# A fused attention and gated-MLP kernel: the first chunk's second half turned by TensorE, and the last chunk's logits in one burst

## The chip, the cores and the metric

The kernel runs on one core of one Trainium2 chip. The metric is the time of one execution on the device in microseconds (us). Engines: PE is TensorE, DVE is VectorE, ACT is ScalarE, POOL is GpSimd, SP is the engine that issues most DMAs here. A q after an engine's name (PEq, SPq) is its instruction queue, which issues DMAs and waits. "Span" is the time in the trace from the first to the last instruction; it is about 1.8 us shorter than the measured time.

Names in the profile: a timeline line gives the output tile first, then its inputs. `lps` are the logits, `e` the exponentials, `eD` their copy in DRAM, `A` the copy loaded back, `m` the mixes, `o` the attention output; `psf<-o,wo` is the output projection, `psf<-hT,wd` the down-projection of the MLP, `psg` and `psu` its gate and up products. "glu" is the gated MLP.

## The reference, cut to what matters

```
x: 2048 x 640 (bf16)
xn = layernorm(x)
q, k, v = xn @ wqkv                    # 32 heads of 20
logits[s, w] = q[s] . k[s - 2 w] / sqrt(20)   for w = 0..7, masked where s - 2 w < 0
o[s] = sum over w of softmax(logits[s])[w] * v[s - 2 w]
out = x + o @ wo + ((xn @ w_gate) * (xn @ w_up)) @ w_down      # inner width 1536
```

Each token attends to eight earlier ones, two apart. The products q*k and A*v are therefore elementwise and run on DVE; the projections and the MLP run on PE.

## The kernel before

The 2048 tokens are cut into four chunks of 512 (numbered 0 to 3), held transposed (features on partitions). A small list scheduler at build time (`Plan`) gives every task an engine, an estimated duration, needs, and a priority; it decides the order on each engine. The order is then fixed.

Chunk 0 has to start fast, so before the change all of it is loaded already transposed, in two halves of 256 tokens. The layer norm statistics of a half are sums over partitions, done by PE with a matrix of ones: S is the sum of x, V the sum of squares of the centred x. (Only here and in "S and V sums" is V this sum; "V's weights", "V starts" and "V of chunk 0" mean the projection to v.)

```
    def feature_sums(what, h, tiles):          # S (what="xt") and V (what="sq") of half h
        ...
            for i in tiles:
                nc.tensor.matmul(st[0]["sum", what, h][:], lhsT=ones[:], rhs=st[0][what, h][:, i, :], ...)

    def center(h, lo, hi): ...                 # DVE: xd = x - mean
    def squares(h, lo, hi): ...                # ACT: xd * xd
    def first(h, j, hi, i=None): ...           # PE: q, k projections of xd (not yet scaled)
    def first_scaled(h, j): ...                # DVE: PSUM * rstd -> q, k
    def normalized(h): ...                     # DVE: xd * rstd -> xnT, for v and the MLP
```

Attention of a chunk: four products of q and k (DVE), four folds (DVE), logits (PE), exponentials (ACT), `e` stored to DRAM and loaded back broadcast over partitions as `A` (the DMA round trip), four mixes A*v and three sums (DVE), then `o` in two DVE operations, then the output projection `outer` on PE. For the last chunk, the logits were made in two bursts, each followed by its own half of `e` and `A`; for the others in one:

```
        for g in range(2):
            if c == NCH - 1:
                add("pe", ("logits", c, g), logits(c, g), 0.45, [("pw", c, 2 * g + 1), ("pw", c, 2 * g), ("sel",)], prio=-100,
                    ring="lg", until=("exp", c, g), slack=0.8)
            elif g == 1:
                add("pe", ("logits", c, 1), lambda: (logits(c, 0)(), logits(c, 1)()), 0.7,
                    [("pw", c, n) for n in range(W // 2)] + [("sel",)], prio=-100,
                    ring=("lg", "aux"), until={"lg": ("exp", c, 0), "aux": ("exp", c, 1)}, slack=0.8)
            add("act", ("exp", c, g), exps(c, g), 0.6, [("logits", c, g if c == NCH - 1 else 1)], prio=-100)
            ...
            add("sp", ("kept e", c, g), keep_e(c, g), 0.65, [done], prio=-100, kb=128)
            add("sp", ("A", c, g), load_a(c, g), 0.65, [("kept e", c, g)] + ([("A", c, 0)] if g else []), prio=-100, kb=512, ...)
```

The softmax here doesn't subtract the row's maximum and nothing guards it: scores larger than these inputs give would overflow.

## Time and profile before

| | before |
|---|---|
| time, median of 3 runs | 258.36 us (258.36 to 258.64) |
| span in the trace | 256.7 us |
| PE busy | 251.0 us, 98% |
| DVE busy | 228.7 us, 89% |
| what PE waited for, in all | 1.0 us |

The page of the kernel before, its busy times and the chain of work that ended last:

```profile
span 256.7 us, 3323 instructions
...
PE 251.0 (98%) x1274; PEld 119.4 (47%) x1297; DVE 228.7 (89%) x233; ACT 110.2 (43%) x203; POOL 31.0 (12%) x55
...
PE 98%; issue 1%; DVE 0%
```

The list of waits of the kernel before, PE only (engine, line, released by whom: us in total, times, longest):

```profile
PE wps L126 <- PEq L844: 0.8, 1, 0.8
PE psf L734 <- issue: 0.2, 1, 0.2
```

PE waits for nobody after its start. The time is the sum of the PE instructions' slots. DVE, busy 89%, sets nothing here. (A slot is the time from one matmul's start to the next one's; the timeline's second column is the modelled duration, which overlaps with the next.)

The timeline of PE at the start of the kernel before. The columns are start, duration, engine, line, operation, output and input, shape, number of instructions:

```profile
8.26 0.49 PE L261 MATMUL sum_sq<-sq,ones 128*128 128x256 bf16 x3
...
9.13 0.71 PE L261 MATMUL sum_xt<-x_115,ones 128*128 128x256 bf16 x5
9.68 0.71 PE L321 MATMUL ps_143<-x_115,wqkv 128*128 128x256 bf16 x5
...
12.95 0.71 PE L261 MATMUL sum_sq<-sq,ones 128*128 128x256 bf16 x5
...
17.87 5.56 PE L443 MATMUL ps<-xnT,wqkv 128*128 128x512 bf16 x24
23.27 1.24 PE L694 MATMUL psg<-xnT,wgu 128*128 128x512 bf16 x5
```

The two groups of five sums at 9.13 and 12.95 are the second half's S and V. From 8.26 to the first gate matmul of the MLP at 23.27 there is no gap.

The timelines of DVE, then of PE, then of SP's DMA issues, at the end of the kernel before:

```profile
215.50 2.82 DVE L624 TENSOR_TENSOR m<-v,A 128x5120 bf16<-128x5120 bf16 x1
...
228.39 2.83 DVE L624 TENSOR_TENSOR m<-v,A 128x5120 bf16<-128x5120 bf16 x1 [2.67 <-DMA A<-eD]
...
242.59 1.49 DVE L643 TENSOR_TENSOR o<-o,R 128x2560 bf16<-128x2560 bf16 x1
```

```profile
218.40 0.40 PE L535 MATMUL lps<-f,sel 128*32 128x512 bf16 x4
233.54 1.24 PE L739 MATMUL psf<-o,wo 128*128 128x512 bf16 x5
247.60 2.75 PE L739 MATMUL psf<-o,wo 128*128 128x512 bf16 x11
```

```profile
219.48 0.57 SPq L556 DMA_DIRECT2D eD<-e  x1
...
224.05 0.56 SPq L568 DMA_DIRECT2D A<-eD  x1
```

DVE already mixes with the first half of A at 215.50, before the second logits at 218.40. It waits 2.67 us for the second half, and still finishes `o` at 244.1, 3.5 us before PE asks for it at 247.60. The two output projections at 233.54 and 247.60 are 14.06 us apart. The same work lies between them in all kernels, so what this distance has over 14.06 is the time that PE waited for `o`.

### The profile page before, as it was taken

The numbers are of one execution on the slowest core, as the hardware profiler recorded it, in microseconds if no ns is written. First come the engines' busy times: TensorE is split into PE (matmuls) and PEld (weight loads), VectorE is DVE, ScalarE is ACT, GpSimd is POOL, SyncE is SP. The second block draws the span as 40 slices with busy tenths as digits, with TensorE's granted clock in tenths as the row PEclk, the third lists the DMA queues.
The fourth block names the chain that finished last, engine by engine and source line by source line (L and its number), as shares of the span: only waits on it lengthen the run. The fifth ranks groups of instructions, "written<-read, shape, count | busy, mean of one in ns | idle before, by whom it ended". The sixth has DMA issues, their size and how long they took to land.

```text
span 256.7 us, 3323 instructions
## 1 busy us (share of the span) xinstructions
PE 251.0 (98%) x1274; PEld 119.4 (47%) x1297; DVE 228.7 (89%) x233; ACT 110.2 (43%) x203; POOL 31.0 (12%) x55
## 2 busy tenths in 40 slices
PE   8999999999999999999999999999999999999994
PEld 4884444444444444444444444444444444444462
DVE  2599999999989999899898999899999999959913
ACT  3516855588755550184555550105555400550000
POOL 0310040000000141223100301302000014000000
PEclk9999999999999999999999999999999999999999
DMA  6993299004570010246350000146002014230003
GB/s 222 414 435 136 111 235 382 17 0 153 182 204 3 0 41 0 82 125 220 113 102 4 0 0 22 54 152 221 11 3 82 0 41 150 82 102 0 23 0 103
DMA packets 16496, 27.11 MB, mean 106 GB/s; under 512 B 9456, under 2 KB 12160, under 8 KB 16096
## 3 DMA queue, kind: packets, MB, share of 16 engines
q1 hardware_dynamic: 13680, 14.98, 18.6%
q0 software_dynamic: 2368, 11.33, 12.0%
q10 hardware_dynamic: 432, 0.59, 0.6%
q8 instruction: 10, 0.16, 0.3%
q14 instruction: 6, 0.05, 0.1%
HBM read 19.16 MB, written 5.77 MB: 97 GB/s over the span
## 4 chain that ended last, share of the span: by engine, by line
PE 98%; issue 1%; DVE 0%
PE ps L443 21%; PE psf L734 20%; PE psg L694 20%; PE psu L694 20%; PE psf L739 8%; PE wps L126 1%; PE lps L535 1%; PE sum_xt L261 1%; PE ps_141 L321 1%; PE ps_143 L321 0%; PE ps_145 L321 0%; PE ps_147 L321 0%; PE ps_279 L321 0%; PE ps_267 L321 0%; PE ps_230 L321 0%
## 5 line engine op out<-in xcount | busy, mean ns | idle before, releaser
L694 PEld LDWEIGHTS <-wgu 128*128 128x128 bf16 x480 | 46.6, 98 | 56.4 <-issue 0.5
L694 PE MATMUL psu<-xnT,wgu 128*128 128x512 bf16 x232 | 59.2, 379 | 0.4
L694 PE MATMUL psg<-xnT,wgu 128*128 128x512 bf16 x238 | 59.5, 379 | 0.1
L734 PE MATMUL psf<-hT,wd 128*128 128x512 bf16 (+1 forms) x247 | 54.0, 369 | 0.4 <-issue 0.2
L624 DVE TENSOR_TENSOR m<-v,A 128x5120 bf16<-128x5120 bf16 x16 | 45.1, 2818 | 2.7 <-DMA A<-eD 2.7
L508 DVE TENSOR_TENSOR pw<-q,k 128x5120 bf16<-128x5120 bf16 (+1 forms) x20 | 45.5, 2277 | 0.3
L443 PE MATMUL ps<-xnT,wqkv 128*128 128x512 bf16 x170 | 39.5, 379 | 0.3
L700 ACT CAST us<-psu 128x512 bf16<-128x512 f32 x48 | 28.1, 586 | 26.8 <-PE psu L694 26.6
L734 PEld LDWEIGHTS <-wd 128*128 128x128 bf16 x252 | 24.3, 98 | 27.5 <-issue 0.8
L700 ACT CAST gs<-psg 128x512 bf16<-128x512 f32 x48 | 28.1, 585 | 19.2 <-PE psg L694 18.8
L634 DVE TENSOR_TENSOR m<-m 128x5120 bf16<-128x5120 bf16 x12 | 33.8, 2819 | 0.1
L443 PEld LDWEIGHTS <-wqkv 128*128 128x128 bf16 x175 | 17.0, 98 | 20.6 <-issue 0.4
L739 PE MATMUL psf<-o,wo 128*128 128x512 bf16 (+1 forms) x103 | 24.1, 369 | 0.1
L714 DVE TENSOR_TENSOR hT<-gs,us 128x512 bf16<-128x512 bf16 x48 | 19.6, 422 | 4.2 <-ACT us L700 4.1
L761 POOL DMA_DIRECT2D out<-osb x15 | 8.2, 549 | 108.1 <-DVE osb L756 108.0
L544 ACT ACTIVATE e<-lps 128x512 bf16<-128x512 f32 x8 | 4.5, 598 | 35.9 <-PE lps L535 35.9
L519 DVE TENSOR_TENSOR pw<-pw 128x2048 bf16<-128x2048 bf16 x16 | 19.5, 1219 | 0.1
L443 PE MATMUL ps<-xnT,wa 128*128 128x512 bf16 x74 | 17.6, 379 | 0.1
L464 ACT CAST v<-ps 128x512 bf16<-128x512 f32 x20 | 11.7, 585 | 12.5 <-PE ps L443 12.5
L739 PEld LDWEIGHTS <-wo 128*128 128x128 bf16 x105 | 10.3, 98 | 11.3
L453 POOL COPY v<-v 128x70 bf16<-128x70 bf16 x3 | 5.9, 1955 | 54.8 <-DVE m L624 54.8
L464 ACT CAST k<-ps 128x512 bf16<-128x512 f32 x15 | 8.8, 586 | 7.8 <-PE ps L443 7.8
(87 smaller groups left out, 173.9 us busy)
## 6 DMA issues: line engine op xcount, KB each, us to landing
A<-eD SPq DMA_DIRECT2D x8, 512.0 KB, 4.7
x_c<-x SPq DMA_DIRECT2D x3, 640.0 KB
wgu<-wgu POOLq DMA_DIRECT2D x1, 1920.0 KB, 11.3
xnD<-x_c SPq DMA_DIRECT2D x3, 640.0 KB, 3.1
wd<-wd POOLq DMA_DIRECT2D x1, 1920.0 KB, 8.1
xr<-xT POOLq DMA_DIRECT2D x15, 128.0 KB, 2.4
out<-osb POOLq DMA_DIRECT2D x15, 128.0 KB, 2.1
wgu<-wgu POOLq DMA_DIRECT2D x1, 1280.0 KB, 8.7
```

The lines of the kernel that those rows point to most:

```text
L443: nc.tensor.matmul(ps[:, 0 : hi - lo], lhsT=weight(b, i), rhs=s["xnT"][:, i, lo:hi], start=(i == 0), stop=(i == KT - 1),)
L464: nc.scalar.copy(dst[:, t, o + lo : o + hi], s["ps", b, lo][:, 0 : hi - lo])
L508: nc.vector.tensor_tensor(s["pw", n][:, :, :, lo:hi], s["q"][:, None, :, lo:hi].to_broadcast([P, 2, KT, hi - lo]), pairs(s["k"][:, :, off ...
L519: nc.vector.tensor_tensor(t[:, :, 0:2, :], t[:, :, 0:2, :], t[:, :, 2:4, :], ALU.add)
L624: nc.vector.tensor_tensor(s["m", n][:], pairs(s["v"][:, :, off : off + CS], DIL), s["A"][:, 2 * n : 2 * n + 2, None, :].to_broadcast([P, 2 ...
L634: nc.vector.tensor_tensor(b[:], a[:], b[:], ALU.add)
L694: nc.tensor.matmul(ps[:], lhsT=wgu[:, f, r, i, :], rhs=st[c]["xnT"][:, i, :], start=(i == 0), stop=(i == KT - 1))
L700: nc.scalar.copy(t[:], st[c]["gps", f, r][:])
L714: nc.vector.tensor_tensor(h[:], st[c]["gu", f, 0][:], st[c]["gu", f, 1][:], ALU.mult)
L734: nc.tensor.matmul(ps[:], lhsT=wd[:, f, m * P : (m + 1) * P], rhs=st[c]["h", f][:, lo:hi], start=(f == 0), stop=False)
L739: nc.tensor.matmul(st[c]["psf", m, lo][:], lhsT=wo[:, t, m * P : (m + 1) * P], rhs=st[c]["o"][:, t, lo:hi], start=False, stop=(t == KT - 1))
L761: eng.dma_start(out=out[c, m, :, lo:hi], in_=st[c]["osb", m][:, lo:hi])
```

## The change

The intent has two parts. First, the second half of chunk 0 is loaded as rows, with its statistics on DVE (`bn_stats`), normalized in place and then turned by ten PE transposes (128 columns each). That removes ten 256-column sums from PE, and takes the PSUM scaling of that half from DVE; its products can start earlier. Second, the last chunk's logits are made in one burst of eight matmuls, which cost less than two bursts of four.

```diff
-        ("sp", nc.sync, ("x0", 1, 0), None, (1, 0, 5), None, 320),
+        ("sp", nc.sync, ("xc", 0), None, None, None, 320),          # rows of the second half, and the identity
...
+    for j in range(KT):
+        add("pe", ("pe C", j), lambda j=j: [first(1, j, n, i) for n in range(2) for i in range(KT)], 1.09,
+            [("turned", 0), ("wb", 2), ("pe v0", 0, 4)], prio=-895 + 0.1 * j, ring="mm", until=("qk1", j), slack=0.3)
+        add("act", ("qk1", j), first_moved(1, j), 0.57 if j < KT - 1 else 0.72, [("pe C", j)], prio=-800)
+
+    def turn_block(k):
+        def emit():
+            ps = (ps_log if k else ps_aux).tile([P, KT, P], BF, name="turned", tag="lg" if k else "aux")
             for i in range(KT):
+                nc.tensor.transpose(ps[:, i, :], st[0]["x", k][:, tcols(i)], st[0]["eye"])
+            st[0]["t", k] = ps
+        return emit
+
+    def turned_moved(k):
+        return lambda: nc.scalar.copy(st[0]["xnT"][:, :, HF + k * P : HF + (k + 1) * P], st[0]["t", k][:])
...
+    for h in range(2):                                               # V of chunk 0, now in halves
+        for t, n in ((0, 2), (2, 2), (4, 1)):
+            add("pe", ("pe v0", h, t), values0(h, t, n), 0.55 * n, [("wv",), ("turned", 0) if h else ("xn0",), ...
...
         for g in range(2):
-            if c == NCH - 1:
-                add("pe", ("logits", c, g), logits(c, g), 0.45, [("pw", c, 2 * g + 1), ("pw", c, 2 * g), ("sel",)], prio=-100,
-                    ring="lg", until=("exp", c, g), slack=0.8)
-            elif g == 1:
+            if g == 1:
                 add("pe", ("logits", c, 1), lambda: (logits(c, 0)(), logits(c, 1)()), 0.7,
-                    [("pw", c, n) for n in range(W // 2)] + [("sel",)], prio=-100,
+                    folded + [("sel",)], prio=-100,
                     ring=("lg", "aux"), until={"lg": ("exp", c, 0), "aux": ("exp", c, 1)}, slack=0.8)
-            add("act", ("exp", c, g), exps(c, g), 0.6, [("logits", c, g if c == NCH - 1 else 1)], prio=-100)
+            add("act", ("exp", c, g), exps(c, g), 0.6, [("logits", c, 1)], prio=-100)
```

(Cut: the removal of the second half's sums, centring and scaling; products and folds of chunk 0 in halves; renamings.) In the order on PE, V's first half and the transposes now come right after the first half's q and k.

## The prediction

> **What bounds the kernel now.** TensorE. The busy table gives PE 251.0 us of a 256.7 us span at full clock; the timeline shows no PE gap from the first sums (3.57 us) to the end of the last output projection (about 253.1). The list of waits has PE waiting 1.0 us in all. DVE is busy 89%, but nobody on PE waits for it. So only two things change the time: the sum of PE instruction slots, and new PE gaps.
>
> **PE slots (start to start in the timeline).** A 128x512 matmul takes 0.216 us (five in 1.08), a 128x256 one 0.109.
> - Removed: the second half's feature sums and sums of squares, 10 x 0.109 = 1.09 us.
> - Added: ten 128x128 transposes. The Trainium skill, "TensorE: Matmul & The Clock Gate", section "Wait — 56ns, not 53.3ns?", gives 55.6 ns for 128 columns; this trace has no such matmul, but its 0.109 and 0.216 fit the same rule. Estimate 0.6 us.
> - V of chunk 0 in halves: 50 x 0.1091 instead of 25 x 0.2158, +0.06 us.
> - Last chunk's logits: two bursts of four cost 0.43 us each; a burst of eight (chunk 1) costs 0.64. Saves 0.2 us.
> Sum: about -0.65 us.
>
> **New gaps at the start.** The second half's S and V sums, and its projections, kept PE busy while weights landed. Now PE wants the third projection block at 9.68 us, but POOL's copies show its weights landing at about 10.0, and V's weights at 11.95; V now comes at about 11.3 instead of 17.9. The new load is 32 KB larger. Estimate: two gaps, 0.75 us together. The row statistics, the transposes and their evictions should just keep up. The glu starts near 23.4 us (before 23.27). Front: about +0.1 after its slots.
>
> **The other engines.** DVE loses the second half's centring, scaling of PSUM and normalizing (6.5 us), gains statistics and one scaling (2.4 us) and about 2 us from folding chunk 0 in halves. It starts chunk 0's products some 4 us earlier, so the scheduler puts logits and down-projections earlier; the PE order shows this. I expect DVE to keep up with small or no PE gaps.
>
> **The end.** Before, the last chunk's first half of A was loaded at 194.6 us, long before its second logits (218.40). Two mixes and a sum ran while the second half travelled; DVE still waited 2.67 us for it (mix at 228.39, 10.0 us after the logits) and finished o at 244.1, 3.5 us before PE asked for it (247.60). Now all four mixes come after the single burst. By PE order, 33.7 us of PE work lies between that burst and the last output projection. The chain is: logits to first A landing 10.0 to 10.9 us; then DVE in its new order, seven 128x5120 ops, o, five gates, one residual, 24.6 us. That is 35.1 us, so PE should stall about 1.4 us before the last output projection.
>
> **Total.** -0.65 + 0.75 + 1.4 = +1.5 us, about 259.9; I lean down a little since landings and gaps may be kinder: 259.4 us, range 257.5 to 261.2. Faster by over 2%: 0.02; within: 0.94; slower: 0.04.
>
> **What would show it.** Gaps on PE at about 9.7 and 11.5 us released by the weight DMA; transposes near 56 ns apart; DVE waiting for A before the last chunk's first mix, at about 224 us; PE waiting 1 to 2 us for o before the last output projection; nothing else idle on PE.
>
> **What would make it wrong.** A landing faster, or the burst earlier on PE than I counted (no end stall: about 258.4); transposes costing 0.1 us or more; PE waiting for folds at the earlier chunks' logits (DVE slack there shrinks to 1 to 3 us); weights landing earlier than POOL's copies suggest.

## The result and the profile after

| | before | after |
|---|---|---|
| time, median | 258.47 us (258.36 to 258.64, 4 runs) | 258.78 us (258.72 to 258.88, 4 runs) |
| ratio, 95% interval | | 1.0012, 0.9995 to 1.0029 |
| span in the trace | 256.7 us | 256.9 us |
| PE busy | 251.0 us | 250.7 us |
| DVE busy | 228.7 us | 227.6 us |

A ratio is the mean time of one kernel's fast runs over the mean of the other's of the same rounds, so it is not quite the ratio of the medians quoted. The time is the same within 2%, and within 0.3%.

The page of the kernel after, busy times and the chain that ended last:

```profile
span 256.9 us, 3403 instructions
...
PE 250.7 (98%) x1299; PEld 121.2 (47%) x1322; DVE 227.6 (89%) x242; ACT 114.1 (44%) x215; POOL 30.2 (12%) x56
...
PE 82%; DVE 10%; DMA 6%; issue 1%; ACT 0%; DVEq 0%; ACTq 0%
```

The list of waits of the kernel after, PE only:

```profile
PE wps L127 <- PEq L873: 0.8, 1, 0.8
PE sum_xt L278 <- DMA x_115<-x: 0.2, 1, 0.2
PE psf L767 <- DVE o L673: 0.2, 1, 0.2
```

The chain is no longer PE alone: it now runs at the start through the loads (the weights of q, k and v have 3.0% of the span) and at the end through DVE's mixes and the DMA of A, and the list of waits names the spot, the last output projection waiting for `o`. The 10% of DVE does not mean that DVE costs 10%; a chain switches engine as soon as a wait is longer than zero. How much the switch cost is only the length of the wait.

The timeline of PE at the start of the kernel after:

```profile
8.23 0.49 PE L278 MATMUL sum_sq<-sq,ones 128*128 128x256 bf16 x3
8.56 0.71 PE L318 MATMUL ps_142<-x_115,wqkv 128*128 128x256 bf16 x5
9.10 0.71 PE L318 MATMUL ps_144<-x_115,wqkv 128*128 128x256 bf16 x5
9.77 0.72 PE L318 MATMUL ps_146<-x_115,wqkv 128*128 128x256 bf16 x5
...
10.87 0.71 PE L318 MATMUL ps_150<-x_115,wqkv 128*128 128x256 bf16 x5
11.72 1.27 PE L493 MATMUL ps<-xnT,wqkv 128*128 128x256 bf16 x10
12.82 0.44 PE L388 MATMUL turned<-x_c 128*128 128x128 bf16 x5
13.10 0.71 PE L493 MATMUL ps<-xnT,wqkv 128*128 128x256 bf16 x5
...
13.93 1.25 PE L493 MATMUL ps<-xnT,wqkv 128*128 128x256 bf16 x10
15.12 0.71 PE L318 MATMUL ps_293<-xnT,wa 128*128 128x256 bf16 x5
...
23.31 1.24 PE L722 MATMUL psg<-xnT,wgu 128*128 128x512 bf16 x4
```

Read starts, not durations. Five 256-column matmuls take 0.545 us, so the block at 9.10 ends at 9.65 and the next should start there: it starts at 9.77, a gap of 0.13 (the third block of weights had not landed). The block at 10.87 ends at 11.42, V starts at 11.72: 0.30 (V's weights). The ten at 13.93 end at 15.02, the second half's projections start at 15.12: 0.10 (they wait for ACT's copy of the second turned block). The five transposes from 12.82 to 13.10 take 0.28 us, 56 ns each. From the squares at 8.23 to the MLP at 23.31 it is 15.08 us, against 15.01 before: without its three gaps it would be 14.55.

The timelines of DVE, then of PE, then of SP's DMA issues, at the end of the kernel after:

```profile
222.90 2.83 DVE L654 TENSOR_TENSOR m<-v,A 128x5120 bf16<-128x5120 bf16 x1 [1.67 <-DMA A<-eD]
...
246.22 1.49 DVE L673 TENSOR_TENSOR o<-o,R 128x2560 bf16<-128x2560 bf16 x1
```

```profile
213.70 0.62 PE L565 MATMUL lps<-f,sel 128*32 128x512 bf16 x8
233.37 1.24 PE L767 MATMUL psf<-o,wo 128*128 128x512 bf16 x5
247.77 2.53 PE L767 MATMUL psf<-o,wo 128*128 128x512 bf16 x11 [0.18 <-DVE o L673]
```

```profile
214.91 1.21 SPq L586 DMA_DIRECT2D eD<-e  x2
218.36 0.56 SPq L598 DMA_DIRECT2D A<-eD  x1
```

`o` is done at 247.71 and the last output projection starts at 247.77. From 233.37 it is 14.40 us, so the stall is 0.34 us (the 0.18 printed counts from the modelled end of the last matmul, which is later than the end of its slot).

The sum: the start costs +0.07 us (15.08 against 15.01: slots -0.46, gaps +0.53), and from the MLP's start to the last output projection +0.13 us (224.46 against 224.33: logits -0.22, stall +0.35). Together +0.20, the difference of the spans; what lies before the squares (8.23 against 8.26) and after the start of the last output projection (9.13 against 9.10) cancels. The PE work fell by about 0.7 us, as intended; about 0.9 us of new waits took its place.

### The profile page after: what moved, and what is told of

Read it like the earlier page. It is cut to its first block, busy times and chain, and to the rows that moved or that the text cites. A ratio compares the mean times of both kernels' runs of the same rounds, so it can differ in the third digit from the quotient of the medians.

```text
span 256.9 us, 3403 instructions
## 1 busy us (share of the span) xinstructions
PE 250.7 (98%) x1299; PEld 121.2 (47%) x1322; DVE 227.6 (89%) x242; ACT 114.1 (44%) x215; POOL 30.2 (12%) x56
## 3 DMA queue, kind: packets, MB, share of 16 engines
q1 hardware_dynamic: 13680, 15.01, 18.4%
## 4 chain that ended last, share of the span: by engine, by line
PE 82%; DVE 10%; DMA 6%; issue 1%; ACT 0%; DVEq 0%; ACTq 0%
PE ps L461 19%; PE psg L722 18%; PE psu L722 18%; PE psf L762 14%; PE psf L767 8%; DVE m L654 4%; DVE m L664 3%; DMA wqkv<-wqkv 3%; PE ps L493 2%; DMA A<-eD 2%; DMA x_115<-x 1%; PE lps L565 1%; DVE hT L742 1%; DVE o L673 1%; DVE o L672 1%
## 5 line engine op out<-in xcount | busy, mean ns | idle before, releaser
L461 PE MATMUL ps<-xnT,wqkv 128*128 128x512 bf16 x145 | 33.8, 379 | 0.4 <-issue 0.2
L461 PEld LDWEIGHTS <-wqkv 128*128 128x128 bf16 x150 | 14.5, 98 | 17.8 <-issue 0.4
L549 DVE TENSOR_TENSOR pw<-pw 128x2048 bf16<-128x2048 bf16 (+1 forms) x20 | 20.1, 1007 | 0.4
L230 DVE BATCH_NORM_STATS2 stats<-x_c 128x6 f32<-128x320 bf16 x28 | 12.0, 470 | 0.8 <-DMA x_c<-x 0.8
L553 DVE TENSOR_TENSOR f<-pw 128x1024 bf16<-128x1024 bf16 (+1 forms) x20 | 11.8, 588 | 1.0
L550 DVE TENSOR_TENSOR pw<-pw 128x1024 bf16<-128x1024 bf16 (+1 forms) x20 | 11.7, 585 | 0.7
```

Source lines behind the costliest of these rows:

```text
L230: nc.vector.bn_stats(s[:, hf, :], xk[:, hf * N2 : (hf + 1) * N2])
L461: nc.tensor.matmul(ps[:], lhsT=weight(b, i), rhs=s["xnT"][:, i, :], start=(i == 0), stop=(i == KT - 1))
L549: nc.vector.tensor_tensor(t[:, :, 0:2, :], t[:, :, 0:2, :], t[:, :, 2:4, :], ALU.add)
L553: nc.vector.tensor_tensor(st[c]["f", n][:, :, lo:hi], t[:, :, 0, :], t[:, :, 4, :], ALU.add)
```

## The experiments

Twelve labels were run (eleven edited kernels, and the changed kernel once more), in three batches, each batch on one chip together with runs of the kernel before. Two things move from one execution to the next and are worth knowing before the traces are compared: the squares start anywhere from 7.89 to 8.83 us, and the gaps for weights differ (below). So a difference of some tenths of a us in one trace is read by stage, not from the total. All gave correct results. The theory after the first comparison: the time is the sum of PE's slots plus three gaps at the start plus the end stall, and the stall is the single burst's cost. The rivals: contention among loads at the start; a DVE that is simply too full; chance.

### First batch: the parts apart (before: 258.69 us median, 258.21 to 260.68, 11 runs)

**e1_split_last: part one alone.** The last chunk's logits in two bursts again.

```diff
-            where, tag = (ps_aux, "aux") if g else (ps_log, "lg")
+            where, tag = (ps_aux, "aux") if g and c < NCH - 1 else (ps_log, "lg")
...
-            if g == 1:
+            if c == NCH - 1:
+                add("pe", ("logits", c, g), logits(c, g), 0.45, [("pw", c, 2 * g + 1), ("pw", c, 2 * g), ("sel",)], ...)
+            elif g == 1:
```

> The changed kernel with the last chunk's logits again in two bursts of four (only part one of the change remains). Theory (PE slots plus two front gaps plus an end stall that the burst makes): the end stall of 0.35 us goes, the second burst's 0.22 us of PE slots comes back, so about 258.65, 0.1 us under the changed kernel; DVE finishes o 2 us or more before the last output projection, and PE waits for no DVE there. Rival (the burst costs nothing, all of the difference is the front): 0.2 us over the changed kernel, 259.0.

Measured: 258.80 us (258.17 to 259.67, 6 runs), ratio to before 1.0001 (0.9973 to 1.0028). The timeline of PE of this kernel:

```profile
233.73 1.24 PE L770 MATMUL psf<-o,wo 128*128 128x512 bf16 x5
...
247.79 5.57 PE L770 MATMUL psf<-o,wo 128*128 128x512 bf16 x29
```

The last output projection comes 14.06 us after the one before it, so there is no stall; `o` is done at 238.70, 9 us early. From the MLP's start to the last output projection it is 224.34 us against 224.46 in the changed kernel: the stall of 0.35 went, and 0.23 for the second burst came back. So the single burst makes the stall, and the two nearly cancel. The rival of a DVE that is simply too full is out: it has the same mixes and sums to do here.

**e2_burst_only: part two alone.** The kernel before with the single burst.

```diff
-            where, tag = (ps_aux, "aux") if g and c < NCH - 1 else (ps_log, "lg")
+            where, tag = (ps_aux, "aux") if g else (ps_log, "lg")
...
-            if c == NCH - 1:
-                add("pe", ("logits", c, g), logits(c, g), 0.45, ...)
-            elif g == 1:
+            if g == 1:
```

> The kernel before with only the single burst in the last chunk. Theory: the burst stays near 218.0 us on PE, where DVE's folds put it; first mix 9.2 us later, DVE then needs 24.7 us less two gates of 0.34, so o is done near 251.2 and PE stalls about 3.8 us before the last output projection: about 262.1 us. The burst is affordable only because part one lets DVE fold earlier. Rival (the burst alone only saves slots): 258.2.

Measured: 265.21 us (264.76 to 265.93, 4 runs), ratio 1.0248 (1.0215 to 1.0281), slower. The timeline of PE, then the engines' busy time in two stretches (us, busy and count for each engine, granted clock, share of DMA, GB/s) of this kernel:

```profile
218.22 0.62 PE L535 MATMUL lps<-f,sel 128*32 128x512 bf16 x8
...
252.55 0.58 PE L736 MATMUL psf<-o,wo 128*128 128x512 bf16 x1 [4.76 <-DVE o L643]
253.36 6.13 PE L736 MATMUL psf<-o,wo 128*128 128x512 bf16 x28 [0.22 <-issue]
```

```profile
248.00:252.00 4.00, 0.00 (x0) 0.00 (x0) 3.93 (x3) 0.00 (x0) 0.00 (x0) 0.99 0.00 0
252.00:256.00 4.00, 3.22 (x9) 1.28 (x10) 1.19 (x2) 0.00 (x0) 0.00 (x0) 0.58 0.00 0
```

The burst starts at 218.22, 4.5 us later than in the changed kernel, because without part one DVE does its last folds later (the last one ends at 215.63 us here, at 210.62 in the changed kernel). PE then waits 4.9 us for `o` (18.98 us between the two projections instead of 14.06). That is the mechanism expected. The size was larger than expected, and the trace shows two reasons for most of it: the first mix came 10.0 us after the burst (228.23), not 9.2; and after the wait the granted clock was 0.58 over the next 4 us (0.50 in each of the first three), so that the last 29 matmuls took about 1.3 us longer. The Trainium skill, "TensorE: Matmul & The Clock Gate", section "What's actually happening", says that an idle window of about 3.4 us puts PE at half clock; here a wait of 4.76 us did it. No wait in the other kernels is that long; the longest, 1.95 us in the late-burst run, left the granted clock at 1.00. So the parts do not add: part one is what makes the burst affordable.

**e3_gate_wgu: are V's weights late because the MLP's weights compete?** The first two loads of the MLP's weights are held until V's weights have landed.

```diff
-        (0, 2, ("wb", 0), lambda: wqkv[:, 1, KT - 1, P - 1 :]),
-        (2, 6, ("wb", 2), lambda: wqkv[:, 4, KT - 1, P - 1 :]),
+        (0, 2, ("wv",), lambda: wqkv[:, 9, KT - 1, P - 1 :]),
+        (2, 6, ("wv",), lambda: wqkv[:, 9, KT - 1, P - 1 :]),
```

> The changed kernel with the first two gate/up weight loads held back until V's weights have landed, so that V's weights have the DMA engines to themselves. PE and DVE orders are the same. Theory (weights set the gap before V at 11.41 to 11.72): V's weights land earlier, the gap shrinks from 0.31 to under 0.1 us, glu starts 0.2 to 0.3 us earlier, total 258.5. Rival (the gap is set by DVE's normalizing, which ends at 11.2): gap stays, 258.8. If the late gate/up weights are late for the glu at 23 us, a gap there shows it.

Measured: 258.81 us (258.36 to 259.63, 6 runs), ratio 1.0005 (0.9977 to 1.0033). The timeline of PE of this kernel:

```profile
10.62 1.81 PE L318 MATMUL ps<-x,wqkv 128*128 128x256 bf16 x15 [0.20 <-DMA wqkv<-wqkv]
12.56 1.26 PE L493 MATMUL ps<-xnT,wqkv 128*128 128x256 bf16 x10
```

V starts 1.94 us after the third block. In the changed kernel it is 1.95 (9.77 to 11.72). The theory of contention with the MLP's loads fell: V's 0.82 MB of weights follow the third block's by the same 1.95 us whether or not those loads run. The rival in the expectation falls too, since DVE's normalizing ended at 11.87 us here, 0.69 before V. The gap is there because PE now asks for V right after the first half's q and k, at 11.4 us instead of 17.87. One rival was not tested: the rows of chunk 1 (640 KB) are issued on the same queue right behind V's weights, and with the MLP's loads held the DMA engines still moved 417 to 436 GB/s from 8 to 11 us.

**e4_early_burst: is the stall set by the place of the burst?** The scheduler's slack for the last burst is lowered so that it comes two groups of five matmuls (2.16 us) earlier.

```diff
-                    ring=("lg", "aux"), until={...}, slack=0.8)
+                    ring=("lg", "aux"), until={...}, slack=-1.4 if c == NCH - 1 else 0.8)
```

> The changed kernel with the last chunk's burst two PE groups (2.16 us) earlier, from 213.70 to about 211.5; DVE's last fold ends at 210.6. Theory: the end stall goes whole (only 0.35 us of the 2.16 can be won), total 258.4; o done about 1.8 us before PE asks. Rival (end not set by the burst): 258.8. If PE has to wait for the fold at the burst, up to 0.2 us comes back there.

Measured: 258.68 us (258.36 to 259.26, 6 runs), ratio 0.9995 (0.9967 to 1.0023). The two projections are 14.06 us apart: no stall, and from the MLP's start to the last one 224.11 us, 0.35 less than the changed kernel. The gain is the stall and no more. The total does not show it, as the third block's weights landed late in this trace (15.55 us from the squares to the MLP). Of the 2.16 us only 0.6 reached `o` (done at 247.10 instead of 247.71): the store for the softmax sums now went ahead of A on SP, and A was issued at 217.61, only 0.75 us earlier.

### Second batch: the start (before: 258.5 us median, 258.05 to 259.07, 11 runs)

**f0_after_again: the changed kernel, not edited.**

> The changed kernel unedited, once more, as the measure for the runs beside it on the same chip. Expected 0.3 us over the kernel before. In the trace: 15.1 us from the first sums of squares to the glu's first matmul, with gaps near 0.3 us before V and 0.1 us before the second half's projections; 224.46 us from there to the last output projection, 0.35 us of it a wait for o.

Measured: 258.98 us (258.77 to 259.79, 6 runs), ratio 1.0026 (1.0012 to 1.0040). The start took 15.08 us as expected; the stall was 0.44 us here. The first comparison gives 0.1% and this one 0.3%; only the second interval is clear of zero.

**f1_split_wv: V's weights in two transfers**, so that the first V blocks need only the first.

```diff
-        ("sp", nc.sync, ("wv",), wqkv, wqkv_in, blocks(5, 10), 800),
+        ("sp", nc.sync, ("wv", 0), wqkv, wqkv_in, blocks(5, 7), 320),
+        ("sp", nc.sync, ("wv",), wqkv, wqkv_in, blocks(7, 10), 480),
...
-            add("pe", ("pe v0", h, t), ..., [("wv",), ...
+            add("pe", ("pe v0", h, t), ..., [("wv",) if h or t else ("wv", 0), ...
```

> The changed kernel with V's weights in two transfers, the two blocks that PE wants first on their own. They land about 1.1 us earlier, so the gap before V (0.31 us) goes. Theory: the gain stops at the next wait. ACT is busy without a break from the second block's root to the eviction of the second turned block, which ends at 15.07 us whatever V does, so the second half's projections still start near 15.1 and the gap before them grows from 0.1 to 0.3 or 0.4 us: sums of squares to glu stays 15.0 to 15.1 us, total unchanged. Rival (the landing of V's weights was the limit of the front): 14.8 us, total 0.3 us less.

Measured: 259.65 us (259.25 to 259.96, 5 runs), ratio 1.0045 (1.0031 to 1.0058). V did start directly after the block before it, so V's gap went. The gap before the second half's projections did not grow as the theory said: it was 0.11 us, against 0.10 in the changed kernel. Since the third block's weights landed late in this trace (a gap of 0.52), the start took 15.17 us in all, and which of the two accounts of the start is right this run does not settle. The time rose: the stall was 0.67 us, and from the start of the last output projection to the end of the span it was 9.47 us, where it is 9.13 in the changed kernel. No expectation had that last one; it is taken up below.

**f2_split_evict: f1, and ACT evicts the second turned block before one of its V copies**, for the gap of 0.10 us.

```diff
-[("t", 0)] if (h, t) == (0, 4) else []
+[("t", 1)] if (h, t) == (0, 4) else []
```

> As the run with V's weights in two transfers, and ACT evicts the second turned block before a V block that nobody waits for. Theory: turned is complete 0.3 us earlier, so now both waits go: sums of squares to glu 14.7 to 14.8 us, total 0.3 us under the changed kernel.

Measured: 259.48 us (259.07 to 260.07, 5 runs), ratio 1.0041 (1.0026 to 1.0056). The start did what was expected: 14.75 us from the squares to the MLP, 0.33 less than the changed kernel (0.13 of it because the third block's weights were not late in this trace). None of it reached the time: the stall was 0.57 us, and the end after the last projection 9.54.

**f3_split_evict_early: f2 with the early burst of e4.**

> Both front edits and the last burst 2.16 us earlier: no end stall. Theory: sums of squares to glu 14.75, glu to last output projection 224.11, so about 0.65 us under the changed kernel and 0.35 us under the kernel before: 258.1 when the kernel before takes 258.45. Rival (gaps at the two ends do not add up): more than 258.4.

Measured: 259.10 us (258.58 to 261.49, 6 runs), ratio 1.0040 (1.0008 to 1.0071). The expected gain was missed. The stall was gone (14.06), but the third block's weights landed late in this trace (15.13 us from the squares to the MLP), and the end was 9.61 us.

### Third batch: the long end, and the two costs by themselves (before: 258.26 us median, 257.90 to 258.46, 9 runs)

**g2_extra_transfer: is one more transfer enough to lengthen the end?** The changed kernel, with the load of the third chunk's rows issued as two transfers; orders on PE and DVE are the same.

```diff
-                nc.sync.dma_start(out=t[:], in_=x[c * CS : (c + 1) * CS, :].rearrange("(p k) d -> p k d", k=CH))
+                src = x[c * CS : (c + 1) * CS, :].rearrange("(p k) d -> p k d", k=CH)
+                for lo in (0, P // 2) if c == 2 else (0,):
+                    hi = P if c != 2 else lo + P // 2
+                    nc.sync.dma_start(out=t[lo:hi], in_=src[lo:hi])
```

> The changed kernel, with the load of the third chunk's rows issued as two transfers by the same queue; nothing else differs, and TensorE's and VectorE's orders are the same. Theory (one transfer more on that queue, by itself, makes the end after the last output projection longer, as in the three split runs): end after the last projection's start 9.5 us instead of 9.1, time about +0.4 us on the changed kernel, 259.2 if that is at 258.8, ratio about 1.003 to 1.004. Rival (it came from the split of V's weights or from chance): end 9.1 us, time as the changed kernel, ratio about 1.001.

Measured: 259.16 us (258.98 to 259.34, 5 runs), ratio 1.0039 (1.0025 to 1.0052). The end was 9.48 us. SP's waits for its last stores, first in the changed kernel, then in this one:

```profile
SPq L880 <- DMA out<-osb: 1.1, 3, 0.5
```

```profile
SPq L883 <- DMA out<-osb: 1.5, 1, 1.5
```

One transfer more on this queue, issued at 31 us, makes SP's final wait one of 1.5 us in place of three that sum to 1.1. (In this trace the stall was 0.11 us, shorter than the changed kernel's, which hides part of it: the span is 257.0.) All four kernels with one more transfer show an end of 9.47 to 9.61 us; all others whose last matmuls ran at full clock show 9.05 to 9.13. So the size is settled: it is the transfer, and not the split of V's weights. Why the last wait depends on the number of transfers is open.

**g1_evict_early: both repairs without an extra transfer.** The eviction order of f2 and the early burst of e4.

```diff
-[("t", 0)] if (h, t) == (0, 4) else []
+[("t", 1)] if (h, t) == (0, 4) else []
...
-                    ring=("lg", "aux"), until={...}, slack=0.8)
+                    ring=("lg", "aux"), until={...}, slack=-1.4 if c == NCH - 1 else 0.8)
```

> The changed kernel with the burst of the last chunk two groups earlier on TensorE (as in the early-burst run) and ScalarE's eviction of the second turned block put ahead of one V block, without the extra weight transfer of the split runs. Theory (the end stall is about 0.35 us and the wait before the second half's projections about 0.10 us, both gone here, and nothing else moves): gated MLP to last output projection 224.1 us without a stall, sums of squares to gated MLP 14.95 to 15.0 us at the same weight landings, span end after the last output projection's start 9.1 us; 258.3 us if the before runs are at 258.5, ratio 0.998 to 1.000 against before. Rival (the extra 0.4 us after the last projection in the split runs comes from the earlier TensorE work and not from the extra transfer): end after the last projection 9.5 us and no gain in time, about 258.7.

Measured: 258.39 us (258.23 to 258.62, 5 runs), ratio 1.0008 (0.9995 to 1.0020). No stall (14.06), 224.11 us from the MLP's start, no wait before the second half's projections, and an end of 9.05 us: all as the theory said. In the profiled run the two weight gaps were 0.39 and 0.30 us, so the start took 15.25 us; with the changed kernel's landings (0.13 and 0.30) it would be 14.99, as expected. The expectation was a tie or a gain of 0.2%; it is a tie, and no version is shown to be faster than the kernel before.

**e5_late_burst: the burst later.**

```diff
-                    ring=("lg", "aux"), until={...}, slack=0.8)
+                    ring=("lg", "aux"), until={...}, slack=3.0 if c == NCH - 1 else 0.8)
```

> The changed kernel with the last chunk's burst of logits one group of ten matmuls (about 1.08 us) later on TensorE. Theory (the time follows the chain burst, exponentials, store and load of A, mixes, sum, gates, residual, which in the changed kernel ends 0.35 us after TensorE asks): the wait before the last output projection grows by 0.7 to 1.1 us to 1.05 to 1.45, time about 259.5 to 259.9, ratio to before 1.004 to 1.006. Rival (the 0.35 us wait is not set by the burst but by VectorE's other work, which would be done in another order): wait stays at 0.3 to 0.5 us, time as the changed kernel.

Measured: 260.94 us (260.41 to 262.62, 4 runs), ratio 1.0117 (1.0087 to 1.0147). The timeline of PE of this kernel:

```profile
216.66 0.61 PE L565 MATMUL lps<-f,sel 128*32 128x512 bf16 x8
234.16 1.24 PE L767 MATMUL psf<-o,wo 128*128 128x512 bf16 x5
...
250.17 5.57 PE L767 MATMUL psf<-o,wo 128*128 128x512 bf16 x29 [1.78 <-DVE o L673]
```

The size in the expectation was a slip of arithmetic: ten 512-column matmuls are 2.16 us, not 1.08. Counted from the MLP's start, the burst came 2.16 us later (192.55 against 190.39), and the stall is 16.01 - 14.06 = 1.95 us, 1.6 more than in the changed kernel. The direction and the mechanism hold (a later burst passes into the stall, less 0.22 us by which A's round trip and 0.33 by which DVE's work up to `o` were shorter in this run), and the rival, a stall that stays at 0.3 to 0.5, is out. The time rose by more than the stall: with f0's ratio the changed kernel would be near 258.9 us on this chip, so about 2 us, of which the stall explains 1.6. For the profiled run the trace has the rest: of the 2.4 us by which its span is longer (259.3 against 256.9), 1.60 are the stall, 0.52 lie before the squares and 0.28 in the start, where the loads landed later. One of the four runs had a lower clock of 0.992. That the edit caused these later landings is not shown.

**e6_double_turn: each transpose issued twice.**

```diff
-                nc.tensor.transpose(ps[:, i, :], st[0]["x", k][:, tcols(i)], st[0]["eye"])
+                for _ in range(2):
+                    nc.tensor.transpose(ps[:, i, :], st[0]["x", k][:, tcols(i)], st[0]["eye"])
```

> The changed kernel with each of the ten transposes of the second half issued twice (the same result). Theory (a transpose takes its slot of 56 ns and nothing else, since both blocks are ready before TensorE asks): five transposes grow from 0.28 to 0.56 us each time, ten more are 0.56 us, of which the 0.10 us wait for the eviction of the second block does not absorb anything as it moves along with the transposes: sums of squares to gated MLP +0.46 to +0.56 us, time about 259.2 to 259.4, ratio to before 1.003. Rival (transposes hide in the gaps around them): below +0.2 us.

Measured: 259.27 us (259.01 to 259.41, 4 runs), ratio 1.0040 (1.0027 to 1.0054). The timeline of PE of this kernel:

```profile
13.09 0.72 PE L389 MATMUL turned<-x_c 128*128 128x128 bf16 x10
13.64 0.71 PE L494 MATMUL ps<-xnT,wqkv 128*128 128x256 bf16 x5
```

Ten transposes take 0.55 us. The start is 15.47 us with gaps of 0.36 us for weights (0.07 and 0.29), so 15.11 without gaps, against 14.55: the ten extra transposes cost 0.56 us, their slots. The expectation erred in one point: the wait of 0.10 us before the second half's projections is gone here, so that much was absorbed, and at equal landings the start would be 0.46 us longer. As it stands it is 0.39, just under the expected 0.46 to 0.56. That the total met its expectation is partly luck: the span is 0.5 us longer than the changed kernel's, of which 0.33 lie before the squares, 0.39 in the start, and -0.22 in a shorter stall.

## Why the prediction was right

The prediction was 259.4 us, with 0.94 for the same within 2%. The measured 258.78 us lies in its range of 257.5 to 261.2. Point by point:

- **What bounds the kernel: right.** PE's slots plus its gaps account for the whole difference of the spans (+0.20 us, worked out above). DVE's busy time fell by 1.1 us and that bought nothing. The prediction's own figures for DVE (6.5 off, 2.4 and 2 added) would have made it 2.1; the difference was not followed up. What the prediction said of DVE ("nobody on PE waits for it") holds after the change too, except at the last output projection.
- **The slots: right.** Predicted -0.65 us, measured about -0.7: -0.46 at the start and -0.22 for the logits. A transpose has a slot of 56 ns (0.28 us for five; 0.56 us for ten more in the doubling run), as the Trainium skill, "TensorE: Matmul & The Clock Gate", section "Wait — 56ns, not 53.3ns?", says for 128 columns.
- **The gaps at the start: right in kind, somewhat large.** Predicted two gaps of 0.75 us together from weights that land late, in the right places. Measured 0.13 and 0.30. A third gap of 0.10 was not foreseen: the prediction said the turned blocks' evictions should just keep up, and the second was late by that much. Together 0.53. These landings move from run to run: the gap before the third block was 0.13 us in the changed kernel, 0.59 in the early-burst run (8.29 to 9.97 us on PE, less two blocks of 0.545), and 0.07 in the doubling run. That the sum is not further off is in part luck: the gap of 0.10 that was not foreseen makes up for some of what the other two fell short.
- **The end stall: right in mechanism, mis-sized.** This is the term that was furthest off. The prediction had 10.0 to 10.9 us from the logits to the first A, and so a stall of 1.4 us. Measured 9.2 us, and a stall of 0.34. The other two terms of that sum held: 33.7 us of PE work was predicted after the burst, and it is 33.73 (247.43, where PE would have asked, less 213.70); 24.6 us of DVE work, and it is 24.8 (222.90 to 247.71). So nearly the whole error sits in the DMA round trip. In the kernel before, from the store of `e` to the issue of A it took 4.57 us (219.48 to 224.05), and the prediction carried over the 10.0 us that contain it; in the changed kernel it took 3.45 us (214.91 to 218.36; both are shown above). Why it differs is open. In the kernel before and in the burst-only run POOL issued the store of an output block within 0.02 us of the store of `e` (219.50 and 219.31), in the changed kernel 3.4 us before it; this is a correlation only and was not tested. (The three runs with the early burst show 4.63 to 4.64 for another reason: there A stands behind the store of the softmax sums in SP's order, and that waits for ACT.) The late-burst run, with 3.45 again and 9.0 us to the first mix, and the burst-only run, with 4.65 and 10.0, show that both values come back. That the round trip sets the stall, the traces show beyond the experiments: seven of them have the burst at the same place on PE (the changed kernel twice, e3, e6, f1, f2, g2), with 8.97 to 9.53 us from the burst to the first mix and stalls of 0.11 to 0.67 us, and in each the stall is that time less 8.86 or 8.87 us.
- **The total.** Predicted -0.65 + 0.75 + 1.4 = +1.5, leaned down to +1.0. Measured -0.7 + 0.53 + 0.35 = +0.2. The answer "same" did not depend on the error: 0.6 us of it are 0.2% of the time.

What the experiments added: the parts of the change do not add up separately. Part one alone ties with before, part two alone loses 2.5%, and both together lose 0.1% in one comparison (an interval that includes none) and 0.3% in the other. Part one gives DVE an earlier start (its first product of chunk 0 at 19.68 instead of 24.21), and that lead is what the single burst uses up.

## What to carry to other kernels

Where one engine is busy 98%, removing work from it pays only if that work was not also covering a load: here 0.7 us of PE slots were removed and about 0.9 us of waits, for weights and for `o`, appeared in their places. Before merging two steps to save issue time, follow the chain from the merged step to its last consumer and compare it with the work that the busy engine has left in between: the two bursts had cost 0.22 us of PE and were buying several microseconds of lead for a DMA round trip. Take the duration of a DMA round trip from several places in the trace and give it as a range; a single one was off by 1.1 us and carried nearly the whole error. (The kernel before shows 3.73 to 4.85 us from the store of `e` to the issue of A in four of its five places, and 17.05 in the fifth, where A was loaded much later than it could be; even the range of the four ends just above the 3.45 measured after.)

## What the Trainium skill lacked or had wrong

- "TensorE: Matmul & The Clock Gate", Part 4 (PE-mode transpose): it gives about 390 ns for a transpose alone and about 275 ns in a kernel, and says that the full clock does not engage for it. Used in a stream of matmuls here, each 128x128 bf16 transpose takes a slot of 56 ns (0.28 us for five, 0.56 us for ten more); the record of a single one is 219 ns long, most of it overlapped by the next. So here they ran at the full clock's slot, between matmuls that kept PE busy; whether transposes alone would, no run shows. That part lacks the slot, which is what a stream pays.
- "DMA: Bandwidth & Descriptors", "Anatomy of one DMA": its fit of 2.0 us plus bytes over 436e3 is for DMAs issued by GpSimd. From it, an estimate for a store of 128 KB is 2.3 us and for a load of 512 KB 3.2 us. On SP's queue, in the trace of the changed kernel, the store of `e` took 3.45 to 4.24 us from its issue to the issue of the load that needs it, and the broadcast load of A 4.0 to 5.3 us from issue to landing (median 4.6). The page has no figure for a store followed by a load of the same data.
- No page has this: one transfer more on SP's queue, far from the end, lengthened the end of the kernel by about 0.4 us (9.47 to 9.61 us against 9.05 to 9.13 after the last output projection's start, in four traces with it against nine without, the burst-only run left out).
